# Attention, FFN and mixture of experts on one core: buffers for converted weights, scaled outputs and keys, the place of an epsilon, and the branches at the end

## The chip, the core and the metric

The kernel runs on one NeuronCore of a Trainium2 chip: a matrix engine (TensorE, PE in the profile; PEld is its weight load), VectorE (DVE), ScalarE (ACT), GpSimd (POOL), and SyncE (SP), which issues most DMAs. Every engine has a queue of its own and works through it in order; an instruction that waits holds everything behind it. The metric is the time of one execution in microseconds on the device. Before the change it is 1440.47 us, the median of three runs.

## The reference

Attention that keeps the 32 largest scores of each row, then an FFN with a squared ReLU, then a mixture of eight experts in which every token goes to two.

```python
# attention: q, k, v are (4, 8, 576, 64)
scores = scale * np.matmul(q, k.transpose(0, 1, 3, 2))
kth = np.partition(scores, -32, axis=-1)[..., -32:-31]
scores = np.where(scores >= kth, scores, -1000000000.0)
attn = np.exp(scores - np.max(scores, axis=-1, keepdims=True))
attn = attn / (np.sum(attn, axis=-1, keepdims=True) + 1e-09)
x = np.matmul(attn, v)                       # as 2304 tokens of 512
# FFN: w_in (512, 2048), w_out (2048, 512)
h = np.maximum(x @ w_in, 0.0)
x = h * h @ w_out
# experts: logits and noise choose two of 8; w1 (8, 512, 1024), w2 (8, 1024, 512)
out[mask] += top2_w[mask, k, None] * (np.maximum(x[mask] @ w1[e], 0.0) @ w2[e])
```

`w_in` and `w_out` arrive as 64-bit floats.

## The kernel before

The program is written with tile pools and a scheduler: the source gives data flow and priorities, the scheduler fixes one order per engine when the program is built. A pool's tile with `bufs=n` has n places, and the n+1st tile waits until the first is no longer read. So a number of buffers changes the order on every engine, not only a wait.

**Attention.** 80 units, each a pair of heads with 128 queries: for each batch b and block i of 128 queries, four pairs j (two in each group g of four heads). 64 units are full and do two rows of scores, one a head; 16 are left-over units (the 64 queries that 576 leaves, both heads in one row of scores), so there are 144 rows of scores. The left-over units stand one by one between full ones, as units 4 to 11, 28 to 35, 40 to 47 and 68 to 75 (counted from 0). A row is made on PE (L355), moved to SBUF on ACT (L358, tile `sb`, 8 buffers), searched on DVE for its 32nd largest (L366 to L373), masked and exponentiated on POOL and ACT (L389 to L395), turned on PE (L406), multiplied by v on PE (L443). `recip` makes the reciprocal of the sum: an epsilon is added on POOL (L400), then DVE inverts (L401). `finish` scales the output on DVE into the tile `x` (L415, L419, two buffers), and ACT and POOL split it into two parts (L420, L421) in `xT`, or in `xL` for left-over units. Keys are loaded and split by `prep_k` into `K4` (four buffers, one a batch and group); `K_AHEAD` says how many units ahead of a batch each of its four halves is made.

**Conversions.** `convert` (L139 to L156) turns one 128x512 part of the FFN's 64-bit weights into two fp32r parts: a load `raw` (L142, two buffers), three passes on ACT, two on DVE (L148, L149), two on POOL (L151, L155), and a store from `csp` (one buffer) to `wsc` in HBM (L156). There are 32, two for each of the FFN's 16 steps, spread over the attention.

**FFN.** Tokens go through in six chunks of three tiles of 128. A chunk is 16 steps: a step loads `wi` and `wo` from `wsc`, does 12 matmuls of 384 columns into `pf` (L285 to L287), squares on ACT, and does 9 matmuls of 512 columns into `acc` (L271 to L273). A chunk can start when the attention of its three tiles is done, and in the first one a step can start when its two conversions are. A rate spreads the steps of a waiting chunk over the units; the scheduler sets the final order. Routing follows each chunk.

**Experts.** After the FFN the eight experts run, loading `raww`, splitting it on ACT and DVE and doing the same two kinds of matmuls (L551 to L572); `y` is scattered to `out` by POOL (L592).

**End.** DVE works out whether any expert got more tokens than its 640 slots (`over`, `most`, `extra`). Every engine loads that number into a register (L877) and branches over the code for the surplus (L878). The function returns `missed`, which says whether the search for the 32nd largest failed in some row; every engine loads it (L911) and branches over a second, slower pass (L912). With these inputs both branches skip.

Of the kernel before, what the change touches and what calls it, by code (L numbers as in the profile page):

```python
# [17 lines left out]
P = 128  # L18
# [7 lines left out]
K_AHEAD = [15, 12, 9, 6]  # L26
# [26 lines left out]
def attention_ffn_moe(ctx: ExitStack, tc: tile.TileContext, q, k, v, w_ffn, w_route, noise, w_exp, out,  # L53
# [85 lines left out]
    def convert(vpool, f, which):  # L139
        n = DM  # L140
        raw = vpool.tile([P, 2 * n], U32, name="raw", bufs=2)
# [11 lines left out]
        sp = vpool.tile([P, 2, n], F32R, name="csp", bufs=1)  # L153
# [257 lines left out]
    def finish(av, rt, dst, j, off, n):  # L411
        x = apool.tile([P, P], F32, name="x")
# [356 lines left out]
    mpool = ctx.enter_context(tc.tile_pool(name="mpool", bufs=2))  # L769
    ps_m = ctx.enter_context(tc.tile_pool(name="ps_m", bufs=2, space=PSUM))  # L770
# [10 lines left out]
    missed = None  # L781
# [22 lines left out]

    opool = ctx.enter_context(tc.tile_pool(name="opool", bufs=1))
    over = opool.tile([P, E], F32, name="over")
    for e in range(E):
        nc.vector.tensor_scalar(over[:, e:e + 1], base[:, e:e + 1], float(-(e * NT + CAP)), 0.0,
                                op0=ALU.add, op1=ALU.max)
    most = opool.tile([P, 1], F32, name="most")  # L810
    nc.vector.reduce_max(out=most, in_=over, axis=mybir.AxisListType.X)
    nc.vector.tensor_scalar(over, over, float(P - 1), None, op0=ALU.add)
    extra = opool.tile([P, E + 1], I32, name="extra")
    nc.vector.tensor_copy(extra[:, 0:E], over)
    nc.vector.tensor_copy(extra[:, E:E + 1], most)
    nc.vector.tensor_scalar(extra[:, 0:E], extra[:, 0:E], 7, None, op0=ALU.logical_shift_right)
    row_i = opool.tile([P, 1], I32, name="row_i")
    nc.gpsimd.iota(row_i, pattern=[[0, 1]], base=CAP, channel_multiplier=1)
    first = opool.tile([P, 1], F32, name="first")
    nc.vector.tensor_copy(first, row_i)  # L820
    far = opool.tile([P, 1], F32, name="far")
    nc.gpsimd.memset(far, float(2 * NT))
# [54 lines left out]
    any_extra = nc.values_load(extra[0:1, E:E + 1], min_val=0, max_val=NT)  # L877
    with tc.If(any_extra > 0):  # L878
        none = mpool.tile([P, ROW], F32, name="mr", bufs=3)
        nc.gpsimd.memset(none, 0.0)  # L880
        nc.vector.tensor_copy(none[:, DM + 3:DM + 4].bitcast(I32), far)
        row = opool.tile([P, 1], F32, name="row")
        for e in range(E):
            nc.vector.tensor_scalar(row, first, float(e * NT), None, op0=ALU.add)
            with tc.For_i(0, (NT - CAP) // P, 1):
                blank(e, row, none)
        for e in range(E):
            nc.vector.tensor_scalar(row, first, float(e * NT), None, op0=ALU.add)
            n_extra = nc.values_load(extra[0:1, e:e + 1], min_val=0, max_val=(NT - CAP + P - 1) // P)
            with tc.For_i(0, n_extra, 1):  # L890
                beyond(e, row)
    return missed
# [81 lines left out]
```

## Time and profile before

| | us |
|---|---|
| median of three runs (1439.49 to 1444.08) | 1440.47 |
| the profiled execution's own time | 1446.42 |
| its span, first to last instruction | 1444.6 |
| PE busy | 1271.8 |
| PEld busy | 1089.4 |
| DVE busy | 941.0 |
| ACT busy | 844.5 |
| POOL busy | 818.4 |

Busy times are unions of instruction spans. The matmuls overlap each other, so a PE that is shown busy need not be at its limit; its weight loads and its count of matmuls say more.

### The profile page before, as it was taken

Reading aid. Unit: us, or ns where it says so; the run is one execution under the profiler, and the core shown is the slowest. Engines: PE = TensorE matmul, PEld = TensorE weight load, DVE = VectorE, ACT = ScalarE, POOL = GpSimd, SP = SyncE. Lnnn points to the kernel's source line nnn. Section 1 sums busy time; section 2 is a strip of 40 time slices with the busy share of each in tenths; the row PEclk is TensorE's granted clock in tenths of the full one; section 3 lists DMA queues with packets and bytes.
Section 4 is the critical chain, followed back from the end, with each engine's and each line's share of the span. In section 5 each row is a group of like instructions: output and inputs, shape, how many; then the busy total and the mean of one; then the engine's idle time right before and its main releaser. Section 6 shows DMA issues by size and latency. Waiting matters only on the chain. (4 is left out here: it accounts for less than half of the span.)

```text
span 1444.6 us, 26379 instructions
## 1 busy us (share of the span) xinstructions
PE 1271.8 (88%) x7937; PEld 1089.4 (75%) x7937; DVE 941.0 (65%) x4944; ACT 844.5 (58%) x1741; POOL 818.4 (57%) x1446
## 2 busy tenths in 40 slices
PE   2566669877699999999999989899899999999995
PEld 1444558665588888878888878788778999999984
DVE  7989999999798489789999100145563434444431
ACT  4677788888687579678788534344453333333320
POOL 4778899888788558748866532615233315134121
PEclk9886679999799999999999999999999999999997
DMA  9964358564436635644632576846564434344231
GB/s 325 365 236 146 129 186 296 183 222 168 157 116 207 228 124 175 220 133 161 218 134 90 194 269 217 270 127 218 191 216 143 144 111 159 121 143 151 86 116 39
DMA packets 85251, 257.60 MB, mean 178 GB/s; under 512 B 10716, under 2 KB 10844, under 8 KB 85088
## 3 DMA queue, kind: packets, MB, share of 16 engines
q1 hardware_dynamic: 75808, 227.32, 47.3%
q0 software_dynamic: 9280, 28.40, 5.5%
q8 instruction: 67, 1.10, 0.3%
q14 instruction: 96, 0.79, 0.2%
HBM read 205.71 MB, written 52.06 MB: 178 GB/s over the span
## 5 line engine op out<-in xcount | busy, mean ns | idle before, releaser
L394 POOL TENSOR_TENSOR sb<-sb,w 128x576 f32<-128x576 f32 x144 | 206.5, 1441 | 23.5 <-ACT w L393 19.8
L367 DVE MATCH_REPLACE8 w<-m,sb 128x96 f32<-128x96 f32 x864 | 201.3, 242 | 0.0
L366 DVE MAX8 m<-sb 128x8 f32<-128x96 f32 x864 | 167.7, 245 | 31.4 <-ACT sb L358 25.7
L592 POOL DMA_INDIRECT out<-y,info x40 | 45.1, 1126 | 244.2 <-DVE y L591 237.6
L576 ACT ACTIVATE ht<-ph 128x384 fp32r<-128x384 f32 (+1 forms) x128 | 56.0, 437 | 215.0 <-PE ph L572 200.2
L577 DVE SCALAR_TENSOR_TENSOR ht<-ph,ht 128x384 fp32r<-128x384 f32 (+1 forms) x128 | 62.6, 489 | 180.2 <-ACT ht L576 161.0
L355 PE MATMUL ps<-K,qt 128*128 128x288 f32 x640 | 133.9, 336 | 41.6 <-ACT sb L358 17.2
L570 PE MATMUL ph<-xe,wi 128*128 128x384 f32 (+1 forms) x512 | 159.5, 312 | 2.8 <-DVE xe L522 2.0
L571 PE MATMUL ph<-xe,wi 128*128 128x384 f32 (+1 forms) x512 | 159.5, 311 | 0.8 <-DVE xe L522 0.8
L572 PE MATMUL ph<-xe,wi 128*128 128x384 f32 (+1 forms) x512 | 158.9, 310 | 0.2 <-DVE wi L564 0.2
L355 PEld LDWEIGHTS ps<-K,qt 128*128 128x128 f32 x640 | 104.4, 210 | 56.4 <-ACT sb L358 24.0
L295 POOL TENSOR_TENSOR gt<-r,gt 128x384 fp32r<-128x384 f32 x96 | 97.7, 1018 | 76.0 <-ACT gt L294 70.5
L406 PE MATMUL pa<-ident,sb 128*128 128x128 f32 x576 | 101.6, 302 | 38.0 <-DVE x L415 14.7
L393 ACT ACTIVATE w<-sb,keep 128x576 f32<-128x576 f32 x144 | 109.6, 772 | 36.2 <-POOL keep L389 35.3
L551 PE MATMUL acc<-wo,ht 128*128 128x512 f32 x320 | 126.7, 398 | 1.8 <-ACT ht L576 1.0
L552 PE MATMUL acc<-wo,ht 128*128 128x512 f32 x320 | 125.4, 394 | 0.0
L395 ACT ACTIVATE sb<-sb,keep 128x576 f32<-128x576 f32 x144 | 111.7, 776 | 22.1 <-POOL sb L394 21.2
L285 PE MATMUL pf<-xT,wi 128*128 128x384 f32 x320 | 113.8, 356 | 11.0 <-DMA wi<-wsc 8.5
L271 PE MATMUL acc<-wo,gt 128*128 128x512 f32 x288 | 117.4, 418 | 5.7 <-DMA wo<-wsc 3.0
L406 PEld LDWEIGHTS pa<-ident,sb 128*128 128x128 f32 x576 | 69.9, 151 | 62.2 <-issue 20.0
L286 PE MATMUL pf<-xT,wi 128*128 128x384 f32 x320 | 110.5, 345 | 3.6 <-POOL xT L421 3.6
L272 PE MATMUL acc<-wo,gt 128*128 128x512 f32 x288 | 112.8, 403 | 0.0
(180 smaller groups left out, 3530.4 us busy)
## 6 DMA issues: line engine op xcount, KB each, us to landing
wi<-wsc SPq DMA_DIRECT2D x96, 512.0 KB
wo<-wsc SPq DMA_DIRECT2D x96, 512.0 KB
raww<-in_exp SPq DMA_DIRECT2D x80, 512.0 KB
raw<-in_ffn SPq DMA_DIRECT2D x32, 512.0 KB
wsc<-csp SPq DMA_DIRECT2D x32, 512.0 KB
xs<-xr SPq DMA_DIRECT2D x40, 258.0 KB
mr<-xs SPq DMA_DIRECT2D x40, 258.0 KB
qn<-in_q SPq DMA_DIRECT2D x40, 256.0 KB
```

Of the source, the lines that this page charges most:

```text
L271: nc.tensor.matmul(acc[tt], gt[:, 0, sl], wo[:, 0, :], start=(f == 0), stop=False)
L285: nc.tensor.matmul(ph[:, 0:n], wi[:, 0, sl], xT[:, 0, c, 0:n], start=(c == 0), stop=False)
L355: nc.tensor.matmul(ps[:, n, 0:HS], st, kt[:, n * HS:(n + 1) * HS], start=(i == 0), stop=(i == len(pairs) - 1))
L366: nc.vector.max(top, sb[:, sl])
L367: nc.vector.match_replace(out=w[:, sl], in_to_replace=top, in_values=sb[:, sl], imm_value=NEG)
L394: nc.gpsimd.tensor_tensor(sb, sb, w, op=ALU.subtract)
L406: nc.tensor.transpose(pt[:, c * P:(c + 1) * P], e[:, c * P:(c + 1) * P], ident)
L551: nc.tensor.matmul(acc[t], hs[i][:, 0, sl], wo[:, 0, :], start=(f == 0), stop=False)
L552: nc.tensor.matmul(acc[t], hs[i][:, 0, sl], wo[:, 1, :], start=False, stop=False)
L570: nc.tensor.matmul(ph[:, 0:n], wi[:, 0, sl], xe[i][:, 0, c, :], start=(c == 0), stop=False)
L571: nc.tensor.matmul(ph[:, 0:n], wi[:, 0, sl], xe[i][:, 1, c, :], start=False, stop=False)
L572: nc.tensor.matmul(ph[:, 0:n], wi[:, 1, sl], xe[i][:, 0, c, :], start=False, stop=(c == NC - 1))
```

## The change

- `raw` gets three buffers and `csp` two, in the first pass; `x` gets four; `K4` gets three instead of four, and the second group of a batch's keys is made 4 and 3 units ahead instead of 9 and 6.
- The epsilon is added on DVE instead of POOL.
- `over`, `most` and `extra` are worked out ahead of the experts in the source, with the load of the condition; `missed` is added to it, so that there is one branch on the way, and the second pass stands inside it, behind the surplus code. The pools are closed ahead of that branch.

```diff
-K_AHEAD = [15, 12, 9, 6]
+K_AHEAD = [15, 12, 4, 3]
...
-        raw = vpool.tile([P, 2 * n], U32, name="raw", bufs=2)
+        raw = vpool.tile([P, 2 * n], U32, name="raw", bufs=3 if keep is not None else 2)
...
-        sp = vpool.tile([P, 2, n], F32R, name="csp", bufs=1)
+        sp = vpool.tile([P, 2, n], F32R, name="csp", bufs=2 if keep is not None else 1)
...
-            K4[b, g] = apool.tile([P, 4, S], F32R, name="K4", bufs=4)
+            K4[b, g] = apool.tile([P, 4, S], F32R, name="K4", bufs=3)
...
-            nc.gpsimd.tensor_scalar(sm, sm, 1.0, EPS, op0=ALU.mult, op1=ALU.add)
+            nc.vector.tensor_scalar(sm, sm, 1.0, EPS, op0=ALU.mult, op1=ALU.add)
             nc.vector.reciprocal(sm, sm)
...
-        x = apool.tile([P, P], F32, name="x")
+        x = apool.tile([P, P], F32, name="x", bufs=4)
...
+    if keep is not None:
+        nc.vector.tensor_tensor(most, most, total[:, 0:1], op=ALU.add)
+    nc.vector.tensor_copy(extra[:, E:E + 1], most)
...
+    any_extra = nc.values_load(extra[0:1, E:E + 1], min_val=0, max_val=NT + P)
+
     todo_e = [(e, PARTS) for e in range(E)]
...
-    any_extra = nc.values_load(extra[0:1, E:E + 1], min_val=0, max_val=NT)
+    wctx.close()
     with tc.If(any_extra > 0):
...
+        if keep is not None:
+
+            again = nc.values_load(missed[0:1, 0:1], min_val=0, max_val=P)
+            with tc.If(again > 0):
+                attention_ffn_moe(tc, q, k, v, w_ffn, w_route, noise, w_exp, out)
...
-        missed = attention_ffn_moe(tc, *args, keep=keep)
-
-        again = nc.values_load(missed[0:1, 0:1], min_val=0, max_val=P)
-        with tc.If(again > 0):
-            attention_ffn_moe(tc, *args)
+        attention_ffn_moe(tc, *args, keep=keep)
```

What the program's order makes of it, at three places. In these rows the numbers behind K and t are the tiles' own, and lines of the changed kernel stand one or more higher than before (L286 there is L285 before).

**SP, the conversions' loads and stores while the first FFN chunk is waited for.** Before:

```order
L156 DMA wsc<-csp 128x1024
L345 DMA qn<-in_q 128x512
L142 DMA raw<-in_ffn 128x1024
L156 DMA wsc<-csp 128x1024
L142 DMA raw<-in_ffn 128x1024
L156 DMA wsc<-csp 128x1024
L345 DMA qn<-in_q 128x512
L142 DMA raw<-in_ffn 128x1024
```

After:

```order
L346 DMA qn<-in_q 128x512
L157 DMA wsc<-csp 128x1024 x2
L143 DMA raw<-in_ffn 128x1024 x2
L157 DMA wsc<-csp 128x1024 x2
L346 DMA qn<-in_q 128x512
L143 DMA raw<-in_ffn 128x1024
L157 DMA wsc<-csp 128x1024
L143 DMA raw<-in_ffn 128x1024
```

Stores and loads stand in pairs there, and more of them between two loads of queries. Counted through the whole order of ACT, the last of the 32 conversions (L154 before, L155 after) stands behind the move of the 68th row of scores before and of the 50th after; when the move of the 43rd row is queued, 17 stand ahead of it before and 25 after.

**PE, behind the weighting with `t_3780`, after 24 units are weighted.** Before:

```order
L443 MATMUL pa<-t_3780,vt 64x128 x2
L406 MATMUL pa<-ident,sb 128x128 x4
L355 MATMUL ps<-K_810,qt 128x288 x4
L406 MATMUL pa<-ident,sb 128x128 x4
L429 MATMUL pa<-ident,lf 128x128
L430 MATMUL pa<-ident,rb 128x128
L355 MATMUL ps<-K_810,qt 128x288 x4
L443 MATMUL pa<-pt,vt 64x128 x8
L285 MATMUL pf<-xT,wi 128x384
L443 MATMUL pa<-t_3941,vt 64x128 x2
```

After, from the fourth block of columns of a step on:

```order
L286 MATMUL pf<-xT,wi 128x384
L407 MATMUL pa<-ident,sb 128x128 x4
L287 MATMUL pf<-xT,wi 128x384
L288 MATMUL pf<-xT,wi 128x384
L274 MATMUL acc<-wo,gt 128x512 x2
L430 MATMUL pa<-ident,lf 128x128
L431 MATMUL pa<-ident,rb 128x128
L274 MATMUL acc<-wo,gt 128x512
L356 MATMUL ps<-K_810,qt 128x288 x4
```

The second head of the unit is turned (L406, L407), the left-over keys and the sums are turned, the next row is scored: FFN matmuls stand between these where attention stood alone. Counted through the whole order of PE, in units scored and units weighted (L443, L444) ahead of a step of the FFN:

| step (chunk, step from 0) | before: scored, weighted | after: scored, weighted |
|---|---|---|
| 0, 1 | 21.0, 17.0 | 21.5, 17.0 |
| 0, 15 | 38.5, 33.0 | 28.5, 24.0 |
| 1, 1 | 42.5, 37.0 | 36.0, 29.8 |
| 1, 15 | 50.5, 45.0 | 46.5, 40.0 |
| 2, 1 | 51.5, 46.0 | 48.5, 42.8 |
| 2, 15 | 60.0, 55.9 | 58.5, 55.0 |
| 3, 0 | 64.5, 59.8 | 64.0, 59.8 |
| 4, 0 | 79.0, 74.0 | 78.5, 73.0 |

From step 10 of chunk 4 on PE's order is the same in both, the experts included.

**POOL, the last rows ahead of the branch and the second load.** Before, with rows of the surplus code left out between the two pieces:

```order
L504 TENSOR_TENSOR info<-info 128x1
L592 DMA out<-y,info 2304x512 x5
L539 DMA cur<-out,info 128x512 x5
L592 DMA out<-y,info 2304x512 x5
L877 TENSOR_LOAD extra
L878 COMPARE_AND_BRANCH
```

```order
L890 UNCONDITIONAL_BRANCH
L878 ISA
L878 UNCONDITIONAL_BRANCH
L911 TENSOR_LOAD keep
L912 COMPARE_AND_BRANCH
```

After:

```order
L505 TENSOR_TENSOR info<-info 128x1
L593 DMA out<-y,info 2304x512 x5
L540 DMA cur<-out,info 128x512 x5
L593 DMA out<-y,info 2304x512 x5
L814 TENSOR_LOAD extra
L880 COMPARE_AND_BRANCH
```

The load of the condition stands last on POOL in both (it does on PE, ACT and DVE too; SP has it early in both). The second load and branch stand inside the code that is skipped.

## Rows read from the trace of the kernel before

**Rows 1.** Busy time by stretch: from:to and length in us, then busy us of PE, PEld, DVE, ACT and POOL (with instructions), the granted PE clock as a share, the DMA engines' share, GB/s.

```profile
0.00:204.00 204.00, 113.89 (x675) 84.95 (x675) 184.22 (x1125) 142.67 (x275) 157.60 (x228) 0.77 0.68 232
204.00:402.00 198.00, 156.97 (x1066) 129.47 (x1065) 184.37 (x1108) 159.41 (x337) 172.38 (x241) 0.91 0.59 203
402.00:622.00 220.00, 216.88 (x1484) 185.46 (x1484) 173.58 (x1146) 166.84 (x359) 157.06 (x293) 1.00 0.54 182
622.00:643.00 21.00, 21.00 (x190) 17.02 (x189) 20.62 (x138) 16.72 (x39) 5.76 (x9) 1.00 0.21 67
643.00:833.00 190.00, 186.51 (x1324) 160.13 (x1322) 149.83 (x1003) 143.41 (x312) 134.86 (x264) 1.00 0.49 165
833.00:945.00 112.00, 102.81 (x526) 89.42 (x526) 9.05 (x33) 45.46 (x89) 45.19 (x96) 0.98 0.74 249
945.00:1427.00 482.00, 473.71 (x2682) 422.94 (x2681) 217.88 (x395) 170.00 (x335) 141.65 (x316) 1.00 0.44 141
```

**Rows 2.** The same for single lines, in the stretches 204 to 402 and 402 to 622. L443 on PE, 20 instructions a unit:

```profile
204.00:402.00 198.00, 28.93 (x382) 21.83 (x380) 0.91 0.59 203
402.00:622.00 220.00, 31.65 (x400) 22.72 (x400) 1.00 0.54 182
```

**Rows 3.** L285 on PE, four a step of the FFN:

```profile
204.00:402.00 198.00, 22.10 (x60) 12.23 (x61) 0.91 0.59 203
402.00:622.00 220.00, 44.01 (x128) 24.08 (x128) 1.00 0.54 182
```

**Rows 4.** L371 on DVE, four a row of scores:

```profile
204.00:402.00 198.00, 27.02 (x142) 0.91 0.59 203
402.00:622.00 220.00, 30.32 (x149) 1.00 0.54 182
```

**Rows 5.** L155 on POOL, one a conversion:

```profile
204.00:402.00 198.00, 25.77 (x19) 0.91 0.59 203
```

**Rows 6.** PE in order of time in the experts, whose matmuls have the widths of the FFN's: start us, duration us, what.

```profile
1418.11 0.34 PE L571 MATMUL ph<-xe,wi 128*128 128x384 f32 x1
1418.29 0.34 PE L572 MATMUL ph<-xe,wi 128*128 128x384 f32 x1
...
1422.34 0.39 PE L551 MATMUL acc<-wo,ht 128*128 128x512 f32 x1
1422.57 0.40 PE L552 MATMUL acc<-wo,ht 128*128 128x512 f32 x1
```

**Rows 7.** Groups of instructions from 0 to 833 us, the conversions on DVE and POOL: busy us, mean ns of one, then idle time of the engine before them and who ended it.

```profile
L149 DVE SCALAR_TENSOR_TENSOR ca<-raw,ca 128x512 uint32<-128x512 uint32 x32 | 37.1, 1160 | 0.1
L148 DVE TENSOR_SCALAR ca<-ca 128x512 uint32<-128x512 uint32 x32 | 21.4, 670 | 0.6 <-ACT ca L147 0.6
L155 POOL TENSOR_TENSOR csp<-ca,csp 128x512 fp32r<-128x512 f32 x32 | 42.7, 1334 | 5.7 <-ACT csp L154 4.5 <-DMA xs<-xr 0.7 <-POOL lf L436 0.4
L151 POOL TENSOR_TENSOR ca<-ca,raw 128x512 uint32<-128x512 uint32 x32 | 41.9, 1311 | 13.9 <-DVE ca L149 8.3 <-issue 2.6 <-POOL sb L394 2.0
```

**Rows 8.** Busy time by stretch again, the second half of the first 204 us, with Rows 1's columns.

```profile
120.00:204.00 84.00, 53.98 (x321) 39.06 (x321) 79.86 (x477) 62.39 (x126) 73.07 (x95) 0.67 0.44 146
```

**Rows 9.** Groups again: the reciprocal L401 on DVE, from 0 to 402 us and then from 402 to 833 us. Last, for the epsilon's add L400 on POOL from 402 to 833 us, what POOL waited for ahead of it (us in total, times; L395 is the exponential on ACT).

```profile
L401 DVE RECIPROCAL sm<-sm 128x2 f32<-128x2 f32 (+1 forms) x38 | 5.6, 151 | 0.6 <-POOL sm L400 0.4
...
L401 DVE RECIPROCAL sm<-sm 128x2 f32<-128x2 f32 (+1 forms) x42 | 6.6, 156 | 13.0 <-POOL sm L400 12.9
...
its engine sat idle before it (us, times) until:
  ACT sb L395: 10.5, 12
```

**Rows 10.** DVE in order of time around two reciprocals: start us, duration us, what.

```profile
208.74 0.22 DVE L401 RECIPROCAL sm<-sm 128x2 f32<-128x2 f32 x2
208.88 0.74 DVE L368 MAX8 m<-w 128x8 f32<-128x576 f32 x1
```

**Rows 11.** Groups again: the scaling of left-over outputs on DVE, from 402 to 833 us.

```profile
L419 DVE TENSOR_TENSOR x<-pa,t 64x64 f32<-64x64 f32 x16 | 3.5, 217 | 8.8 <-POOL xT L421 8.2 <-PE pa L443 0.3
```

**Rows 12.** Waits over the whole span: who waited for whom, us in total, times, longest; then, of line L323, the splitting of keys on POOL: duration ns min/median/max, first and last start.

```profile
PE ps L355 <- POOL K L323: 13.8, 1, 13.8
...
L323 POOL TENSOR_TENSOR K<-kn,K x14: 2615/2632/2798, 27.9 to 400.7; 64x1152 fp32r<-64x1152 f32 x14
```

**Rows 13.** The last 20 us by line, sequencers with a q: duration ns min/median/max, first and last start in us. The scatters, the first load and branch, the second load and branch, and the closing barrier.

```profile
L592 POOL DMA_INDIRECT out<-y,info x5: 972/983/1027, 1426.0 to 1434.2; - x5
L877 POOLq TENSOR_LOAD <-extra x1: 758/758/758, 1434.2 to 1434.2; - x1
L878 POOLq COMPARE_BRANCH  x1: 53/53/53, 1435.0 to 1435.0; - x1
L878 POOLq EVENT_SEMAPHORE  x6: 17/30/43, 1438.1 to 1438.5; - x6
L878 POOLq INC_SWDGE_SEM  x1: 388/388/388, 1438.6 to 1438.6; - x1
L911 POOLq TENSOR_LOAD <-keep x1: 312/312/312, 1439.0 to 1439.0; - x1
L912 POOLq COMPARE_BRANCH  x1: 50/50/50, 1439.4 to 1439.4; - x1
L912 POOLq EVENT_SEMAPHORE  x6: 17/30/43, 1441.9 to 1442.4; - x6
L906 POOLq DRAIN  x3: 40/107/898, 1442.9 to 1444.3; - x3
```

More of the change, by code (lines that the diff above doesn't have):

```diff
@@ L768, in attention_ffn_moe @@
     actx.close()
-    mpool = ctx.enter_context(tc.tile_pool(name="mpool", bufs=2))
-    ps_m = ctx.enter_context(tc.tile_pool(name="ps_m", bufs=2, space=PSUM))
+    mpool = wctx.enter_context(tc.tile_pool(name="mpool", bufs=2))
+    ps_m = wctx.enter_context(tc.tile_pool(name="ps_m", bufs=2, space=PSUM))
     after.append(ps_m)
@@ L779, in attention_ffn_moe @@
     step(10 ** 6)
-    missed = None
     if keep is not None:
@@ L793, in attention_ffn_moe @@
         nc.vector.tensor_copy(missed, total[:, 0:E])
+    over = cpool.tile([P, E], F32, name="over")
+    for e in range(E):
+        nc.vector.tensor_scalar(over[:, e:e + 1], base[:, e:e + 1], float(-(e * NT + CAP)), 0.0,
+                                op0=ALU.add, op1=ALU.max)
+    most = cpool.tile([P, 1], F32, name="most")
+    nc.vector.reduce_max(out=most, in_=over, axis=mybir.AxisListType.X)
+    nc.vector.tensor_scalar(over, over, float(P - 1), None, op0=ALU.add)
+    extra = cpool.tile([P, E + 1], I32, name="extra")
+    nc.vector.tensor_copy(extra[:, 0:E], over)
+    if keep is not None:
+        nc.vector.tensor_tensor(most, most, total[:, 0:1], op=ALU.add)
+    nc.vector.tensor_copy(extra[:, E:E + 1], most)
+    nc.vector.tensor_scalar(extra[:, 0:E], extra[:, 0:E], 7, None, op0=ALU.logical_shift_right)
+    row_i = cpool.tile([P, 1], I32, name="row_i")
+    nc.gpsimd.iota(row_i, pattern=[[0, 1]], base=CAP, channel_multiplier=1)
+    first = cpool.tile([P, 1], F32, name="first")
+    nc.vector.tensor_copy(first, row_i)
+    far = cpool.tile([P, 1], F32, name="far")
+    nc.gpsimd.memset(far, float(2 * NT))
+    any_extra = nc.values_load(extra[0:1, E:E + 1], min_val=0, max_val=NT + P)
     todo_e = [(e, PARTS) for e in range(E)]
@@ L802, in attention_ffn_moe @@
             pass
[L805 to L822, printed above, removed]
     def blank(e, row, rows):
@@ L875, in beyond @@
                                      bounds_check=NT - 1, oob_is_err=False)
-    any_extra = nc.values_load(extra[0:1, E:E + 1], min_val=0, max_val=NT)
+    wctx.close()
     with tc.If(any_extra > 0):
[L879 to L892, printed above, removed]
+        with tc.tile_pool(name="opool", bufs=1) as opool, tc.tile_pool(name="mpool2", bufs=2) as mpool, \
+                tc.tile_pool(name="ps_m2", bufs=2, space=PSUM) as ps_m, \
+                tc.tile_pool(name="ps_acc2", bufs=2, space=PSUM) as ps_acc:
+            none = mpool.tile([P, ROW], F32, name="mr", bufs=3)
+            nc.gpsimd.memset(none, 0.0)
+            nc.vector.tensor_copy(none[:, DM + 3:DM + 4].bitcast(I32), far)
+            row = opool.tile([P, 1], F32, name="row")
+            for e in range(E):
+                nc.vector.tensor_scalar(row, first, float(e * NT), None, op0=ALU.add)
+                with tc.For_i(0, (NT - CAP) // P, 1):
+                    blank(e, row, none)
+            for e in range(E):
+                nc.vector.tensor_scalar(row, first, float(e * NT), None, op0=ALU.add)
+                n_extra = nc.values_load(extra[0:1, e:e + 1], min_val=0, max_val=(NT - CAP + P - 1) // P)
+                with tc.For_i(0, n_extra, 1):
+                    beyond(e, row)
+        if keep is not None:
+            again = nc.values_load(missed[0:1, 0:1], min_val=0, max_val=P)
+            with tc.If(again > 0):
+                attention_ffn_moe(tc, q, k, v, w_ffn, w_route, noise, w_exp, out)
 def build(shapes):
```

7 lines of the change are left out of this document (4 added, 3 removed).

## The prediction

> **What bounds the kernel now.** I read the table of busy time by stretch first [rows 1], because the page's mean over the span (PE busy 1271.8 of 1444.6 us) mixes stages with different limits. The cuts are where PE's lines change: attention and conversions alone to 204 us; chunk 0 of the FFN with attention and conversions to 402; chunks 1 and 2 with attention to 622; attention alone to 643; chunks 3 and 4 with what is left of attention to 833; the last chunk to 945; the experts to 1427; the end. Divide each busy time by its stretch. To 402 us DVE is at 90 and 93% while PE is at 56 and 79%: DVE sets the pace. From 402 to 622 PE is at 99%, its weight loads at 84%, and DVE falls to 79%, 46 us idle (220 − 173.6). The weight loads show that this PE is really at its limit: the experts, where PE does nothing but matmuls of the FFN's widths, have 88% (422.9 of 482), the last FFN chunk 80%. From 622 to 643 DVE is at 98%. So the attention alternates between two limits, and its loss is the 46 us in which DVE, the pacemaker of most of the stage, is starved behind FFN matmuls.
>
> For the working I need prices. A step of the FFN is 12 matmuls of 384 columns and 9 of 512. Such matmuls start 0.18 and 0.23 us apart [rows 6], so a step takes PE 12 × 0.18 + 9 × 0.23 = 4.2 us. From 402 to 622 us PE did 128/4 = 32 steps [rows 3] and 400/20 = 20 units [rows 2]; what the steps leave, 220 − 134, makes 4.3 us of PE a unit. A conversion costs DVE (37.1 + 21.4)/32 = 1.83 us and POOL (42.7 + 41.9)/32 = 2.65 us [rows 7]. From 204 to 402 DVE did 142/4 = 35.5 rows of scores [rows 4] and 19 conversions [rows 5] in 184.4 us busy, so (184.4 − 34.8)/35.5 = 4.2 us a row; from 402 to 622 it is 173.6/37 = 4.7. I take 4.4. A full unit, two rows, thus costs DVE twice what it costs PE, and every FFN step costs PE alone.
>
> **Conversion buffers: the order.** The second `csp` and third `raw` add no instruction. What they remove directly is small: POOL waits 5.7 and 13.9 us ahead of its two passes, most of it for ACT and DVE, 0.7 for a store [rows 7]. Their real effect is the order. Conversions end at the 50th row instead of the 68th, so the steps of chunk 0 are no longer spread thin by missing weights, and the three chunks' places among the units move (table of steps in the section on the change). Chunk 3 begins at 64 units scored and 59.8 weighted in both. Up to that point, 643 us now, the work of every engine is the same; only how well it overlaps can change. So I compare each chunk's need of PE and of DVE between its step 1 and its end: PE 15 steps × 4.2 and 4.3 a unit weighted; DVE 4.4 a row, rows being twice the units scored less one per left-over unit, and 1.83 a conversion.
>
> Before: chunk 0, PE 132 against DVE 173; chunk 1, 97 against 62; chunk 2, 106 against 75. PE's excess is 35 + 31 = 66 us, and the trace shows 46 of DVE idle: 20 were absorbed by rows of scores already queued in the 8 `sb` buffers. After: chunk 0, 63 + 7 × 4.3 = 93 against 7 units (55) and about 10 conversions (18), 73; chunk 1, 107 against 79; chunk 2, 115 against 88. The excess is 20 + 28 + 27 = 75 us, no less than before, but in three pieces with stretches between them in which DVE is behind and the queue refills. With 10 absorbed by each, 45 remain against 46, a gain of 1; with 20 in each of two and none in the third, 35 remain, a gain of 11. The gap between chunks 1 and 2 is only 2 units, too short to fill the queue, so I take a value near the small end: **−4 us**. The bounds: 20 absorbed in all, as now, gives 75 − 20 − 46 = +9; 20 in each of three gives 15 − 46 = −31.
>
> **Epsilon on DVE.** 80 instructions leave POOL and join DVE. The trace has no such one on DVE; the nearest is the reciprocal on the same tile. The next instruction starts 0.07 us after the second of two that began together [rows 10], and the recorded duration of 0.15 us [rows 9] is the upper bound. Before 402 us, with DVE saturated, 38 of them add 38 × 0.07 = 2.7 (at most 5.7) and remove only 0.4 us of waiting for POOL. After 402 the 42 others add 2.9 and face 12.9 us of waits for POOL's add. But POOL was itself idle ahead of that add for 10.5 us, waiting for the exponential on ACT [rows 9]; that wait now stands on DVE, at the same place in its queue, with the searches of later rows behind it as before. Some 2.4 us are really removed, and DVE has slack there. **+2 us**, from −8 (2.3 − 10, if all the waits vanish and DVE sets the time) to +5.3.
>
> The row that decides this is DVE's 95% from 120 to 204 us with 0.4 us of waiting for POOL's add. The Trainium skill, "Perfetto Trace Analysis", section "Optimizing Scalar/DVE Operations", speaks against this part: it says that where DVE is saturated, work may be worth moving off it, even to GpSimd. To 402 us the trace agrees (90 to 93% busy, 0.4 us of waits); from 402 to 622, at 79%, its condition isn't met. Taken over all 80, the rule would make this term +5.6 and the forecast 1436.1, beside rival A.
>
> **`x` with four buffers.** The scaling of left-over outputs waits 8.2 us for POOL to release `x` between 402 and 833 us [rows 11]. That lies in stretches where PE is at 99 and 98%; from 402 to 622 only 3.1 us of PE idle can come back. **−2 us**, from −8.2 to 0.
>
> **`K4` with three buffers.** The same splits and loads are made, those of a batch's second group later, at 4 and 3 units ahead. The split may not write its buffer before the last scores that read it are done, so POOL's L323, and what is queued behind it there (masking, conversions), could wait on PE. A unit costs DVE 8.8 us, so 3 units are 26 us of lead and 4 are 35, against two POOL passes of 2.63 us each [rows 12] with the load ahead of them on SP's queue. That covers it: **0**. If the cover is gone, PE stands as it did once at the start, 13.8 us for that same line [rows 12]. Three batches follow another, and in each some 10 of those 13.8 us would still be hidden by the rows queued in `sb` (8 rows, 35 us of DVE), so 3 × 3 = 9 is the upper end: 0 to +9.
>
> **The end.** After the last scatter POOL loads `extra` and branches at 1435.0, and comes out at 1438.1; then the second load, branch and exit take from 1438.6 to 1441.9 [rows 13]. The change leaves one load and one branch. From 1438.1 to 1441.9 is 3.8 us: **−4 us**. If the exit's bookkeeping stays (0.9 us from 1438.1 to 1439.0) and the longer jump takes half a microsecond more, −2.4; if the one branch costs no more and its tail shrinks too, −5. The condition isn't really loaded early: on POOL its load still stands last, behind the scatters, so its 0.76 us stay. DVE's few operations on `over` move ahead of the experts' code; DVE is at 45% there (217.9 of 482 [rows 1]) and hides them.
>
> **Sum.** −4 + 2 − 2 + 0 − 4 = −8 us. The profiled execution takes 1446.42 itself, so 1438.4; it lies 5.95 above the median of the runs, which brings the forecast to 1432.5.
>
> **Rivals.** A: only the end gains. The attention's terms cancel, since the PE excess is as large after as before (75 against 66) and the epsilon takes what `x` gives. Then −4, 1436.5, within 0.3% of before (4.3 us, about what a measurement of this kernel can tell from no change). For it: the same work up to unit 64. Against it: the refills.
>
> B: the spare time really goes. If the three pieces are absorbed so well that half of DVE's 46 idle microseconds vanish, −23 − 4 gives 1413.5. For it: from 204 to 402 us PE idles 41 us that earlier steps could use. Against it: in the chunks that follow, PE is asked for more than DVE in each.
>
> C, slower: POOL becomes the bound ahead of chunk 0. When the 43rd row is moved, 25 conversions are done instead of 17: 8 × 2.65 = 21 us more for POOL in front of 204 us. From 120 to 204 POOL has 84 − 73.1 = 11 us left [rows 8], at its 87% beside DVE's 95%. What doesn't fit, 10 us, delays masking, then the turning and weighting behind it; DVE can't regain it, as it paces the stage. With the end's −4 and nothing else gained it is +6, 1446.5. It decides if POOL is filled to 97% or more there and DVE's waits name POOL's lines. Against it: a conversion done there is not done later, and POOL's idle time before 120 us is larger (157.6 of 204 busy).
>
> D, that the branch's condition is not loaded early, is what the order shows, and costs nothing against the sum, which doesn't count on it.
>
> **How the numbers follow.** Forecast, 1422 to 1436: 0.42. A, 1436 to 1445: 0.23. B, below 1422: 0.15. C or a late `K4`, above 1445: 0.20. So faster by more than the bound 0.57, the same 0.23, slower 0.20. The range of 8 in 10 goes from B's price, 1414, to C's, 1447, which leaves about 0.08 below and 0.10 above.
>
> **What would show it.** In the changed kernel's table by stretch, DVE's idle time up to the start of chunk 3 should be near 42 us, in three pieces, and chunk 3 should start some 4 us earlier than 643. The reciprocal should show its waits on ACT's exponential through the epsilon's add, not none. L323 should wait for no scores, and PE for no keys apart from the start. The tail behind the last scatter should be 4 us shorter, with one branch on POOL. The experts, in the same order on PE, should last 482 us. The forecast is wrong if DVE's idle time halves (B), if POOL passes 97% ahead of chunk 0 (C), or if the stretch from chunk 3 to the experts, 302 us now, moves by more than 5, as I have nothing there that changes its work.

## The result, and the profile after

The changed kernel takes 1418.22 us (median of four runs, 1416.5 to 1420.39) where the kernel before took 1442.09 beside it: a ratio of 0.9836, interval 0.9812 to 0.986, 24 us faster. The forecast was 8 us faster. The direction was right, the size three times too small; of the rivals, B (1413.5) came nearest. Two single runs further down (one of keys_eps, one of late_conversions_beside) took several per cent longer at a lower granted clock, and their kernels' medians leave them out.

The profiled execution takes 1419.02 us itself, 27.4 less than the profiled one before (1446.42). First the table of busy time by stretch, cut where the chunks begin and end: up to chunk 0, chunk 0, attention alone, chunk 1, a short gap, chunk 2, attention alone. Columns as in [rows 1]. Before:

```profile
0.00:210.00 210.00, 118.44 (x702) 89.07 (x703) 190.22 (x1167) 147.91 (x287) 162.72 (x239) 0.77 0.68 232
210.00:382.00 172.00, 135.27 (x907) 112.09 (x907) 162.84 (x966) 139.98 (x294) 154.52 (x208) 0.91 0.63 220
382.00:409.00 27.00, 24.14 (x190) 19.39 (x190) 22.36 (x147) 19.71 (x43) 19.20 (x32) 0.90 0.16 52
409.00:506.00 97.00, 93.88 (x630) 81.62 (x629) 71.11 (x475) 71.35 (x154) 69.65 (x132) 1.00 0.60 197
506.00:511.00 5.00, 5.00 (x29) 4.32 (x27) 0.95 (x7) 3.00 (x9) 2.79 (x9) 1.00 0.80 256
511.00:620.00 109.00, 109.00 (x756) 91.57 (x756) 94.51 (x618) 85.57 (x184) 76.43 (x139) 1.00 0.50 172
620.00:651.00 31.00, 29.63 (x244) 24.75 (x243) 28.72 (x198) 25.72 (x56) 14.13 (x34) 1.00 0.36 120
sum 651.00, PE 515.36 PEld 422.80 DVE 570.72 ACT 493.25 POOL 499.43; mean PE 73.62 PEld 60.40 DVE 81.53 ACT 70.46 POOL 71.35
```

After:

```profile
0.00:224.00 224.00, 121.72 (x719) 93.77 (x720) 209.42 (x1170) 160.91 (x309) 173.17 (x228) 0.78 0.73 248
224.00:317.00 93.00, 88.06 (x568) 74.72 (x568) 90.87 (x519) 78.08 (x169) 84.87 (x111) 0.98 0.84 287
317.00:348.00 31.00, 28.76 (x254) 23.64 (x250) 30.72 (x213) 24.77 (x55) 17.28 (x33) 1.00 0.26 84
348.00:462.00 114.00, 108.91 (x767) 93.53 (x766) 104.31 (x686) 89.92 (x189) 89.75 (x147) 1.00 0.58 193
462.00:477.00 15.00, 11.59 (x80) 9.15 (x79) 13.08 (x89) 14.27 (x33) 14.37 (x27) 0.84 0.40 136
477.00:592.00 115.00, 112.69 (x819) 96.22 (x818) 105.47 (x689) 92.24 (x199) 82.81 (x142) 0.99 0.46 154
592.00:623.00 31.00, 29.04 (x242) 24.27 (x241) 30.63 (x222) 27.25 (x61) 18.91 (x40) 1.00 0.34 108
sum 623.00, PE 500.76 PEld 415.30 DVE 584.50 ACT 487.41 POOL 481.15; mean PE 71.54 PEld 59.33 DVE 83.50 ACT 69.63 POOL 68.74
```

Read the third busy column, DVE's, against the length of each stretch. Chunk 1 of before is the hole: 97 us, 26 of them without DVE. After, it is 10 of 114. Over the whole way to chunk 3, DVE is idle 651 − 570.7 = 80 us before and 623 − 584.5 = 38 us after, 42 less; and it works 14 us more. 42 − 14 = 28 us is how much earlier chunk 3 begins. The work done by then isn't quite the same. L371 (L372 after) on DVE, four a row of scores, from 0 to the start of chunk 3, before, then after:

```profile
0.00:651.00 651.00, 87.17 (x452) 0.90 0.59 201
```

```profile
0.00:623.00 623.00, 84.94 (x445) 0.91 0.62 209
```

That is 113 rows before and 111 after. Two rows, some 9 us of DVE (an estimate, at the prediction's 4.4 us a row), are left for later, so not all of the 28 us is gain. The granted clock is no rival in the hole: it is 1.00 in chunk 1 in both tables.

The squaring on POOL (L295 before, L296 after), one a step, marks the steps of chunks 3 to 5: times are first and last start. Before, then after:

```profile
L295 POOL TENSOR_TENSOR gt<-r,gt x48: 991/1012/1039, 650.7 to 941.5; 128x384 fp32r<-128x384 f32 x48
```

```profile
L296 POOL TENSOR_TENSOR gt<-r,gt x48: 996/1013/1033, 623.1 to 920.2; 128x384 fp32r<-128x384 f32 x48
```

Chunk 3 begins 27.6 us earlier, but the last step comes only 21.3 earlier: 6.3 us are given back in chunks 3 to 5, to which those two rows were left. The tail, from the last scatter's start to the span's end, was 1444.6 − 1434.2 = 10.4 us [rows 13] and is now 1417.2 − 1411.8 = 5.4. POOL's instructions there, by line, as in [rows 13]:

```profile
L593 POOL DMA_INDIRECT out<-y,info x5: 971/980/1028, 1404.4 to 1411.8; - x5
```

```profile
L814 POOLq TENSOR_LOAD <-extra x1: 507/507/507, 1411.0 to 1411.0; - x1
```

```profile
L880 POOLq COMPARE_BRANCH  x1: 53/53/53, 1411.6 to 1411.6; - x1
```

There is one load and one branch, and the load still comes last in POOL's order.

**What makes DVE work more.** The groups of DVE, different shapes apart, over the whole span: the epsilon's addition (L401) and the reciprocal behind it (L402).

```profile
L401 DVE TENSOR_SCALAR sm<-sm 128x2 f32<-128x2 f32 x64 | 36.8, 575 | 4.1 <-ACT sb L396 3.9
L402 DVE RECIPROCAL sm<-sm 128x2 f32<-128x2 f32 x64 | 9.6, 149 | 0.2
L402 DVE RECIPROCAL sm<-sm 128x1 f32<-128x1 f32 x16 | 2.4, 148 | 0.0
L401 DVE TENSOR_SCALAR sm<-sm 128x1 f32<-128x1 f32 x16 | 2.2, 139 | 1.3 <-ACT sb L396 1.3
```

On the same tile the reciprocal takes 0.15 us in either shape; the addition takes 0.14 with one element a row and 0.575 with two. Where one of these goes is seen in order of time, first DVE, then POOL (start us, duration us, what):

```profile
202.39 0.21 DVE L372 MAX8 m<-cand 128x8 f32<-128x56 f32 x1
202.52 1.28 DVE L401 TENSOR_SCALAR sm<-sm 128x2 f32<-128x2 f32 x1
203.71 0.08 DVE L374 MATCH_VALUE_LOAD cand<-m 128x8 f32 x1
```

```profile
202.48 1.28 POOL L324 TENSOR_TENSOR qt<-qn,qt 128x512 fp32r<-128x512 f32 x1
203.72 1.28 POOL L152 TENSOR_TENSOR ca<-ca,raw 128x512 uint32<-128x512 uint32 x1
```

POOL began 0.04 us ahead, and DVE's addition ends at 203.80, just behind POOL's end at 203.76. A longer one, of 3.5 us, lies beside POOL instructions in close succession. The wait is inside the instruction, so no table of waits shows it, only its duration. All of them counted: 35 of the 64 additions of two elements took 0.25 us or more. All 35 began while a POOL instruction ran, and 34 of them end 0.02 to 0.03 us behind the end of one. To the start of chunk 3 the additions take 29.6 us, more than the 14 us by which DVE works more; the two rows that it hasn't done yet are some 9 us of the difference.

### The profile page after: what moved, and what is told of

Same layout as the page of the kernel before. It is cut to its first block, busy times and chain, and to the rows that moved or that the text cites. A ratio compares the mean times of both kernels' runs of the same rounds, so it can differ in the third digit from the quotient of the medians.

```text
span 1417.2 us, 26382 instructions
## 1 busy us (share of the span) xinstructions
PE 1261.8 (89%) x7937; PEld 1085.0 (77%) x7937; DVE 970.6 (68%) x5025; ACT 844.6 (60%) x1741; POOL 798.2 (56%) x1366
## 3 DMA queue, kind: packets, MB, share of 16 engines
q1 hardware_dynamic: 75808, 227.32, 48.5%
## 5 line engine op out<-in xcount | busy, mean ns | idle before, releaser
L395 POOL TENSOR_TENSOR sb<-sb,w 128x576 f32<-128x576 f32 x144 | 207.6, 1448 | 17.8 <-ACT w L394 14.5
L577 ACT ACTIVATE ht<-ph 128x384 fp32r<-128x384 f32 (+1 forms) x128 | 55.9, 437 | 216.5 <-PE ph L573 216.5
L356 PE MATMUL ps<-K,qt 128*128 128x288 f32 x640 | 133.6, 335 | 40.1 <-POOL K L324 15.9
L296 POOL TENSOR_TENSOR gt<-r,gt 128x384 fp32r<-128x384 f32 x96 | 97.8, 1019 | 63.6 <-ACT gt L295 57.7
L407 PE MATMUL pa<-ident,sb 128*128 128x128 f32 x576 | 99.4, 297 | 36.2 <-DVE x L416 13.0
L286 PE MATMUL pf<-xT,wi 128*128 128x384 f32 x320 | 115.4, 361 | 13.3 <-ACT r L292 5.8
L287 PE MATMUL pf<-xT,wi 128*128 128x384 f32 x320 | 111.9, 350 | 4.8 <-POOL xT L422 4.8
L272 PE MATMUL acc<-wo,gt 128*128 128x512 f32 x288 | 112.8, 403 | 3.0 <-DMA wo<-wsc 1.5
L407 PEld LDWEIGHTS pa<-ident,sb 128*128 128x128 f32 x576 | 68.2, 149 | 60.8 <-issue 22.8
L273 PE MATMUL acc<-wo,gt 128*128 128x512 f32 x288 | 111.0, 396 | 0.0
```

Source lines behind the costliest of these rows:

```text
L272: nc.tensor.matmul(acc[tt], gt[:, 0, sl], wo[:, 0, :], start=(f == 0), stop=False)
L286: nc.tensor.matmul(ph[:, 0:n], wi[:, 0, sl], xT[:, 0, c, 0:n], start=(c == 0), stop=False)
L356: nc.tensor.matmul(ps[:, n, 0:HS], st, kt[:, n * HS:(n + 1) * HS], start=(i == 0), stop=(i == len(pairs) - 1))
L395: nc.gpsimd.tensor_tensor(sb, sb, w, op=ALU.subtract)
L407: nc.tensor.transpose(pt[:, c * P:(c + 1) * P], e[:, c * P:(c + 1) * P], ident)
```

## The experiments

Each kernel was timed beside the kernel before; kernels timed together, beside the same runs of the kernel before, are a set, and have the same time in the last column. The changed kernel's own ratio came out 0.9836, 0.9827 and 0.989 in three sets (24, 23 and 16 us faster), so figures of one set are compared with each other, and others only with 0.6% (9 us) of room.

| run | median us | ratio to before | interval | before, us |
|---|---|---|---|---|
| undo_conv | 1453.8 | 1.0056 | 1.0035 to 1.0078 | 1446.4 |
| undo_eps | 1413.5 | 0.978 | 0.9762 to 0.9797 | 1446.4 |
| eps_tt | 1432.1 | 0.9906 | 0.9889 to 0.9923 | 1446.4 |
| undo_end | 1433.8 | 0.9916 | 0.9899 to 0.9933 | 1446.4 |
| changed_again | 1419.2 | 0.9827 | 0.9802 to 0.9852 | 1442.4 |
| undo_x | 1419.2 | 0.9832 | 0.9808 to 0.9855 | 1442.4 |
| eps_by_column | 1399.1 | 0.9692 | 0.9669 to 0.9716 | 1442.4 |
| conv_and_keys | 1412.8 | 0.9784 | 0.9762 to 0.9807 | 1442.4 |
| keys_only | 1438.3 | 0.9989 | 0.9973 to 1.0004 | 1440.0 |
| keys_csp | 1424.0 | 0.9883 | 0.9859 to 0.9907 | 1440.0 |
| late_conversions | 1418.0 | 0.9832 | 0.9805 to 0.986 | 1440.0 |
| keys_eps | 1451.6 | 1.0082 | 1.0061 to 1.0103 | 1440.0 |
| changed_beside | 1429.4 | 0.989 | 0.9863 to 0.9918 | 1445.7 |
| undo_end_beside | 1432.8 | 0.9926 | 0.9898 to 0.9954 | 1445.7 |
| eps_tt_beside | 1430.5 | 0.9911 | 0.9882 to 0.9941 | 1445.7 |
| keys_eps_by_column | 1435.6 | 0.9936 | 0.9914 to 0.9959 | 1445.7 |
| conv_and_keys_beside | 1414.8 | 0.9812 | 0.9792 to 0.9831 | 1441.6 |
| late_conversions_beside | 1419.5 | 0.9841 | 0.9819 to 0.9863 | 1441.6 |

The theory: the conversion buffers' order fills the hole in chunk 1, and the epsilon on DVE is a cost. The rivals: the gain is the waits taken from DVE (for `x`, for POOL's add), or the later keys.

### The conversion buffers and the keys

```diff
# undo_conv, from the changed kernel
-        raw = ... bufs=3 if keep is not None else 2)
+        raw = ... bufs=2)
-        sp = ... name="csp", bufs=2 if keep is not None else 1)
+        sp = ... name="csp", bufs=1)
```

> The changed kernel with the conversion buffers of before (raw 2, csp 1); epsilon on VectorE, x, K4 and the end as changed. In the program's order chunk 0 is spread again over units 21.5 to 37.5 scored, as before the change. Theory (the order that the conversion buffers give is what gained): most of the gain is lost, 1436 to 1446 us, VectorE idle again 70 to 85 us up to the start of chunk 3. Rival 1 (the gain is the waits taken from VectorE by x with four buffers and by the epsilon leaving GpSimd): 1418 to 1426 us, the reciprocal's, x's and sb's waits still gone.

Slower than before. The cut at its chunks shows the hole again, 103 us with 78.5 of DVE (chunk 1, then the gap and chunk 2):

```profile
406.00:509.00 103.00, 100.67 (x665) 85.89 (x666) 78.47 (x533) 75.64 (x165) 70.88 (x128) 0.98 0.58 190
509.00:519.00 10.00, 8.74 (x69) 7.38 (x66) 2.39 (x14) 6.72 (x15) 3.48 (x10) 1.00 0.53 171
519.00:630.00 111.00, 108.94 (x740) 91.77 (x738) 97.58 (x644) 85.78 (x181) 79.32 (x130) 0.98 0.50 165
```

DVE's idle time up to chunk 3 is 662 − 588.6 = 73 us. It was worse than I expected: with `x`, keys, end and epsilon as changed it is 7 us behind before, so the rest of the change without these buffers is a loss. It also answers the rival. In chunk 1 of the kernel before, the largest idle times of DVE do name POOL, for `x` and for the epsilon's add (us in total, times, longest):

```profile
DVE x L419 <- POOL xT L421: 8.2, 1, 8.2
DVE sm L401 <- POOL sm L400: 5.6, 2, 5.3
DVE rs L236 <- PE pf L222: 5.5, 1, 5.5
DVE m L366 <- ACT sb L358: 3.9, 3, 2.4
```

In undo_conv neither is there, and the hole is as large (24.5 us without DVE, 26 before the change); DVE waits for scores, for outputs and for the exponential instead:

```profile
DVE m L367 <- ACT sb L359: 8.7, 5, 2.6
DVE x L420 <- PE pa L444: 5.3, 2, 3.8
DVE sm L401 <- ACT sb L396: 4.5, 2, 4.0
DVE x L416 <- PE pa L444: 3.3, 3, 1.4
```

```diff
# conv_and_keys, from the kernel before (keys_only: the first and last pair alone;
# keys_csp: without raw)
-K_AHEAD = [15, 12, 9, 6]
+K_AHEAD = [15, 12, 4, 3]
-        raw = ... bufs=2)
+        raw = ... bufs=3 if keep is not None else 2)
-        sp = ... name="csp", bufs=1)
+        sp = ... name="csp", bufs=2 if keep is not None else 1)
-            K4[b, g] = ... bufs=4)
+            K4[b, g] = ... bufs=3)
```

> The kernel before with the conversion buffers and the keys' change alone (the buffers don't fit without the space that the third K4 buffer less frees). Chunk 0 lies at units 22 to 34 scored. Theory (this order is what gained): VectorE's idle time to the start of chunk 3 falls from 80 to 45 to 60 us; 1415 to 1428 us where before is 1442. Rival (the gain needs x or the epsilon's place too): over 1432.

> The kernel before with the keys' change alone (three K4 buffers, later halves). Chunk 0 stays spread (units 22 to 37.5), chunk 1 lies at 40.5 to 48. Theory (the conversion buffers' order gains, the keys only make room for them): 1436 to 1446 us where before is 1442, VectorE idle 65 to 80 us up to chunk 3, no wait of PE for keys beyond the one at the start. Rival (the keys' later splitting relieves GpSimd and is itself the gain): under 1430.

> The kernel before with the keys' change and two csp, raw still two. Chunk 0 lies at units 21.5 to 32, chunk 1 at 36.5 to 48. Theory (the order is what counts, and csp makes it): about the time of conv_and_keys, 1409 to 1420 us. Rival (three raw buffers are needed): over 1428.

The keys alone change nothing measurable (0.9989); with the buffers it is 0.9784, more than the whole change gives. Two `csp` without the third `raw` give about half of it, 0.9883, above the time I had set for "csp makes it" and under that for "raw is needed": both buffers seem to count (the third `raw` alone was not run). The keys' part is that they make room: the conversion buffers alone don't fit into SBUF beside four `K4`. In keys_only, chunk 1 is the same hole; in conv_and_keys it is mostly filled (one row each):

```profile
393.00:491.00 98.00, 96.51 (x639) 81.81 (x639) 64.30 (x423) 70.09 (x150) 69.91 (x132) 1.00 0.60 200
```

```profile
359.00:466.00 107.00, 104.81 (x751) 90.27 (x750) 91.88 (x608) 86.98 (x184) 93.36 (x162) 1.00 0.63 208
```

PE does its 16 steps in either. The first has 64 us of DVE beside them, the second 92. That is not the whole gain. In the two profiles chunk 3 begins 10 us earlier (638.5 and 628.4), and chunks 3 to 5 take another 10 us less (293 and 284); by the start of chunk 3 the one has done 112 rows of scores and the other 113. Why so much of the gain lies behind chunk 3 stays open.

```diff
# late_conversions, late_conversions_beside: conv_and_keys with
-CONVERT_LATER = 1000
+CONVERT_LATER = 3000
```

> conv_and_keys (same buffers throughout) with the conversions' priority lowered (CONVERT_LATER 3000 for 1000), so that the order is again more like that of before: chunk 0 at units 21.5 to 35, chunk 1 at 39.5 to 47, chunk 2 at 49.5 to 58.5. Theory (order): part of the gain goes though no buffer is taken away, 1420 to 1434 us, VectorE idle 55 to 70 us to chunk 3. Rival (the buffers' removed waits are the gain): 1410 to 1416.

> conv_and_keys with the conversions' priority lowered; no buffer differs. Theory (the order gains): 5 us or more above conv_and_keys_beside, VectorE idle 10 us more to the start of chunk 3, mostly in chunk 1. Rival (the removed waits gain): within 3 us of it.

> conv_and_keys once more, beside late_conversions: ratio to before 0.977 to 0.985.

The first result lies under the theory's span and over the rival's, and had no conv_and_keys in its set. Side by side the same buffers in the later order are 4.7 us slower, with intervals that overlap a little. DVE's chunk 1 is 103 us with 80.7 busy, against 107 with 91.7:

```profile
376.00:479.00 103.00, 101.95 (x699) 87.29 (x700) 80.74 (x537) 80.01 (x173) 81.39 (x150) 1.00 0.63 208
```

```profile
359.00:466.00 107.00, 104.65 (x750) 90.15 (x749) 91.73 (x609) 86.82 (x185) 92.98 (x160) 1.00 0.64 210
```

DVE idles 22 us in the first and 15 in the second. The lost time shows only behind the attention's three chunks, in L295 (first and last start), late_conversions_beside first:

```profile
L295 POOL TENSOR_TENSOR gt<-r,gt x48: 996/1014/1030, 624.0 to 913.8; 128x384 fp32r<-128x384 f32 x48
```

```profile
L295 POOL TENSOR_TENSOR gt<-r,gt x48: 996/1014/1086, 626.7 to 909.1; 128x384 fp32r<-128x384 f32 x48
```

With the later order chunk 3 begins no later, but DVE has done 111 rows by then where the other has done 113, and chunks 3 to 5 take 290 us where the other takes 282. So the order alone moves time in the theory's direction, but this step back towards the old order takes only a fifth of the gain. Late_conversions and keys_only, whose chunk 1 lies over 7.5 units each, are still 20 us apart in one set. How much of that is the finer order on the engines and how much a wait that the second buffers take from POOL, ACT or SP, these runs don't separate. There is such a wait: ACT stands before L154 for the store from `csp` 6.7 us in keys_only (4.6 in the kernel before), and not at all in conv_and_keys.

### The epsilon

```diff
# undo_eps, from the changed kernel
-            nc.vector.tensor_scalar(sm, sm, 1.0, EPS, op0=ALU.mult, op1=ALU.add)
+            nc.gpsimd.tensor_scalar(sm, sm, 1.0, EPS, op0=ALU.mult, op1=ALU.add)
# eps_tt, eps_tt_beside: ep is a constant tile of epsilons
+            nc.vector.tensor_tensor(sm, sm, ep[:, 0:sm.shape[1]], op=ALU.add)
# eps_by_column; keys_eps_by_column does the same to keys_only
+            for c in range(sm.shape[1]):
+                nc.vector.tensor_scalar(sm[:, c:c + 1], sm[:, c:c + 1], 1.0, EPS, ...)
# keys_eps: keys_only with the change's own line for the epsilon
```

> The changed kernel with the epsilon back on GpSimd. The order changes with it: chunk 0 lies at units 22 to 34 scored, half-way between before and after. Theory (order gains, and the epsilon on VectorE is a cost because its instruction lasts 0.49 us in the mean, up to 3.5, as it ends with whatever GpSimd is doing): VectorE busy falls by some 35 us over the attention, the half-way order gives some of that back: 1412 to 1424 us. Rival 1 (taking the wait for GpSimd's add from VectorE is a gain): over 1428 us, with the reciprocal waiting 10 us or more for GpSimd.

> The changed kernel with the epsilon added on VectorE one column at a time (128x1 twice for a full unit). In the changed kernel's trace all 16 additions of 128x1 took 154 ns or less and those of 128x2 up to 3.5 us. If it is the form with two elements a row that waits for GpSimd, every addition takes 0.13 to 0.17 us, VectorE's busy time falls by some 20 us and the time by 3 to 15 us against the changed kernel (the order moves somewhat: chunk 0 ends at unit 30.5 instead of 28.5). Rival (128x1 escaped by chance): mean of an addition 0.3 us or more, time as the changed kernel or above.

> The kernel before with the keys' change and the epsilon on VectorE as changed, order as before (chunk 0 at 21.5 to 37.5, chunk 1 at 42.5 to 50.5). Theory (the epsilon's addition holds VectorE up to the end of GpSimd's instruction): 5 to 20 us slower than keys_only, mean of an addition 0.3 to 0.5 us. Rival (leaving GpSimd is worth the 13 us of waits ahead of the reciprocal): 3 to 13 us faster than keys_only.

> The kernel before with the keys' change and the epsilon on VectorE by columns; order near that of before (chunk 0 at 21.5 to 36, chunk 1 at 39.5 to 48.8). If the epsilon's only cost on VectorE is the hold: at least 10 us under keys_eps's ratio of 1.008 and no slower than keys_only, ratio 0.985 to 0.999. If the additions themselves weigh on VectorE: 1.003 or more.

In undo_eps the reciprocal waits 8.3 us for POOL again, and the kernel, whose order has moved too, is still faster than the changed one (0.978 against 0.983 to 0.989). In keys_eps, with an order like that of before, the move costs 13.3 us against keys_only in the same set. By columns it costs nothing: keys_eps_by_column is at 0.9936, and eps_by_column is 20 us faster than the changed kernel beside it, 0.9692 against 0.9827, the best kernel here. Its additions, by groups:

```profile
L402 DVE TENSOR_SCALAR sm<-sm 128x1 f32<-128x1 f32 x144 | 20.2, 140 | 5.4 <-ACT sb L396 5.2
```

144 instructions of one element take 20.2 us; 64 of two and 16 of one took 39. Of the 144, 114 began while a POOL instruction ran, and none took more than 0.156 us. DVE's busy time up to chunk 3 is 570.1 us there, as before the change, and chunk 3 begins at 609. The part of the 20 us that comes from the order, which moves a little (chunk 0 ends at unit 30.5), isn't told apart.

> The changed kernel with the epsilon on VectorE as the sum of two tiles (tensor_tensor with a constant tile of epsilons) in place of a tensor_scalar; the order on the engines stays that of the changed kernel up to chunk 4. If the 0.49 us belong to the tensor_scalar form, which waits for a running GpSimd instruction, the mean falls to 0.15 us, VectorE's busy time by 27 us and the time by 5 to 20 us: 1398 to 1413 us. If every small VectorE instruction behind the softmax waits so, nothing changes: 1415 to 1421 us.

> The changed kernel with the epsilon as a sum of two tiles on VectorE. If this form is held by GpSimd just as the tensor_scalar is and the 10 us were the chip: 0 to 3 us from changed_beside. If the form itself costs: 8 us or more above it.

The sum of two tiles is held as well, and in the shape that the tensor_scalar escapes. I expected 0.15 us; it is 0.47 in either shape, and the time is that of the changed kernel (1.1 us above it in the same set):

```profile
L403 DVE TENSOR_TENSOR sm<-sm,ep 128x2 f32<-128x2 f32 x64 | 30.3, 474 | 3.3 <-ACT sb L398 3.2
```

```profile
L403 DVE TENSOR_TENSOR sm<-sm,ep 128x1 f32<-128x1 f32 x16 | 7.4, 465 | 0.9 <-ACT sb L398 0.9
```

### `x` and the end

```diff
# undo_x, from the changed kernel
-        x = apool.tile([P, P], F32, name="x", bufs=4)
+        x = apool.tile([P, P], F32, name="x")
# undo_end, undo_end_beside: the end as before, the rest as changed
-    any_extra = nc.values_load(extra[0:1, E:E + 1], min_val=0, max_val=NT + P)
...
+        missed = attention_ffn_moe(tc, *args, keep=keep)
+        again = nc.values_load(missed[0:1, 0:1], min_val=0, max_val=P)
```

> The changed kernel with x in two buffers. The order is the same on every engine; only the wait for a free x can come back. If x was a small term (the 8.2 us of waiting before lay where PE set the pace): 0 to 4 us above the changed kernel. Rival (x is a main part of the gain, since VectorE's queue stands behind that wait): 8 to 15 us above it, with the wait of left-over scalings for GpSimd back at 8 us or more.

> The changed kernel with the end of before: two loads and two branches, the surplus numbers worked out behind the experts. The order of attention and FFN is that of the changed kernel. If the end is worth what the tail of the profile shows (10.4 us from the last scatter to the end before, 5.4 after): 1423 us, 4 to 6 above the changed kernel. Rival (the second branch is hidden by the landing of the last scatter): 1418 to 1420 us.

> The changed kernel with the end of before. If only the tail differs: 4 to 6 us above changed_beside. If working out the surplus numbers ahead of the experts matters too: 9 us or more above it.

> The changed kernel itself once more, so that the others of this call have it beside them on the same chip. Ratio to before 0.980 to 0.987.

> The changed kernel, beside the three others on one chip: ratio to before 0.980 to 0.987.

`x` is worth nothing: 1419.16 us against 1419.20, and the 8.2 us of [rows 11] don't come back with two buffers in the new order. The end's first run had no changed kernel beside it and seemed to say 12 us; that was the difference between sets. Beside the changed kernel it is 3.5 us, which the intervals don't separate from nothing, and the tail in the profiles, 10.6 us against 5.5, says 5.

## Why the prediction was right in direction and wrong in size

**The order of the conversions: −4 predicted, −27 to −30 measured** (conv_and_keys in two sets). This is the step that failed: "The excess is 20 + 28 + 27 = 75 us, no less than before", with 10 us absorbed by each piece. PE's side was right: 93, 107 and 115 us reckoned for chunks 0 to 2, 93, 114 and 115 measured. DVE's side was not: 73, 79 and 88 reckoned, 91, 104 and 105 busy in the table above, so 21 us idle and not 45. I had counted its rows by PE's order, as units scored between a chunk's step 1 and step 15. L372, four a row, counts what DVE did in the three chunks:

```profile
224.00:317.00 93.00, 13.54 (x71) 0.98 0.84 287
348.00:462.00 114.00, 16.11 (x88) 1.00 0.58 193
477.00:592.00 115.00, 17.21 (x85) 0.99 0.46 154
```

That is 17.8, 22 and 21.3 rows where I had 12.5, 18 and 20: 10.5 rows at 4.4 us, 46 us of work that was there to be done. The rest of the 61 us by which DVE was busier than reckoned is the epsilon's additions, 16 us in the three chunks (L401):

```profile
224.00:317.00 93.00, 5.77 (x9) 0.98 0.84 287
348.00:462.00 114.00, 6.54 (x13) 1.00 0.58 193
477.00:592.00 115.00, 3.68 (x11) 0.99 0.46 154
```

Some of the rows wait in the queue when a chunk begins. That is the absorption, which I put at 10 us a piece by choice and not from a row; the rows alone make it 15 a piece, towards the end of the range that I gave ("20 in each of three"). Two counts of rows were slips besides: by the table of steps chunk 0 after holds seven full units, 14 rows or 62 us and not 55, and chunk 1 before holds 13 rows or 57 us and not 62. Put right, the excess is 68 us after against 71 before, and the conclusion would hardly have changed. Nor is it true that up to chunk 3 "the work of every engine is the same": DVE has done two rows fewer. I also compared only 402 to 622 us, and left out the 34 of the 80 idle us that lie elsewhere before chunk 3. So the sign that I named, an idle time "near 42 us", was met by the 38 measured through luck: it was reckoned from the 46 us of one stretch, and the figure to hold beside it is 80. The experiments show that the buffers, with the keys to make room, are what gains (undo_conv, keys_only, conv_and_keys). That the order is a part of it rests on one small difference (late_conversions_beside); how large a part is not shown.

**Epsilon: +2 predicted, some +13 measured** (keys_eps against keys_only; the changed kernel lies 20 above eps_by_column). The sign was right, and so was the guess that the reciprocal's wait would turn into one for ACT: the changed kernel's addition waits 5.2 us for the exponential in all. The price was not. I took the reciprocal as the nearest row for a 128x2 instruction, and gave 0.15 us as the upper bound. In [rows 7] stood the warning: L148, a tensor_scalar, has a mean of 670 ns, and its median in that trace is 432. And there was a nearer row: the cast L246 on DVE, 128x2 as well, took from 0.154 to 1.320 us in the kernel before, 0.169 in the median. The Trainium skill, "SBUF — State Buffer", section "Who interferes with whom", has the rule that I did not weigh: a VectorE instruction in a two-port mode, which tensor_scalar can enter, or with two inputs in SBUF beside a GpSimd instruction that reads SBUF, uses the port pair that it shares with GpSimd, and whichever starts second waits for the whole of the other. The traces agree for the two forms that are held: 0.575 us for the tensor_scalar of two elements, 0.47 for the tensor_tensor. That the reciprocal (0.15) and the tensor_scalar of one element (0.14) escape is what the traces show. No run here shows the port itself.

**`x`: −2 predicted, 0 measured. Keys: 0 predicted, 0 measured**; PE's waits for L324 are 15.9 us in two, against 13.8 in one [rows 12]. **The end: −4 predicted, −5 by the profiles**, −3.5 by the times; its load was indeed not early.

**Chunks 3 to 5:** 297 us instead of 291. Here I had nothing. A part is the two rows that DVE had not done by the start of chunk 3. The held additions don't explain it: the stretch takes 291 us in eps_by_column, which has none, but also 290 in keys_eps and 289 in undo_conv, which have them, and 299 in keys_eps_by_column, which has none. Otherwise the cause stays open.

**The rivals.** B gave DVE 23 us of its idle time back; it is 42, less 14 of added work. That B's price came within 5 us of the measured time is in part luck: it is the sum of a larger gain and a cost that B doesn't have. C is refuted: POOL is at 89% from 120 us to chunk 0. In the set of changed_again the whole change gives −23 and conv_and_keys −30; with −5 for the end, +12 is left for the epsilon and `x`, near the 13 of keys_eps.

## What to carry to other kernels

Where two engines take turns as the bound, count for each stretch what the starved engine really did there, in its own instructions, and price a change of order by the work that it puts beside the other engine's long stretch; a second buffer on a side path can be worth 2% where the waits that it removes are a few microseconds, as it changes the order on every engine too. To say how much is the order, change the order alone; here that moved 5 us of 27. When a small instruction moves to VectorE beside a busy GpSimd, look for a row of the same operation and shape, compare its mean with its median, and prefer a form that isn't held. Parts of one change can have opposite signs: here, in one set, the whole gave 23 us, the buffers with the keys by themselves 30, and the whole with the epsilon added by columns 43.

## What was not expected of the hardware

That a tensor_scalar of 128x2 lasts up to 3.5 us beside GpSimd while one of 128x1 never passes 0.16 us in 144, so that two instructions of half the size are faster than one; and that the reciprocal, on the same tile of two elements, is never held (0.17 us at most in 80, of which 64 have two elements).
